# Gated linear attention into a star-ReLU feed-forward layer: two sets of PSUM banks for the attention blocks, and another listed order

## The chip, the core and the metric

The kernel runs on one core of a Trainium2 chip. The metric is the device time of one execution in microseconds (us). A core has engines that run side by side, each with its own queue in order: TensorE (PE in the profile, its weight loads PEld), VectorE (DVE), ScalarE (ACT), GpSimd (POOL), and SyncE (SP), which here issues nearly all DMAs. TensorE writes its products to PSUM, which has eight banks of 512 float32 per partition; VectorE and ScalarE read them from there.

## The reference

Two parts follow one another. The first is a recurrence over 768 tokens for 4 batches and 8 heads of 48 channels; the second is a feed-forward layer over the 3072 tokens of the first one's output.

```python
for t in range(S):
    state = alpha[:, :, t, :, None] * state + np.einsum('bhd,bhe->bhde', k[:, :, t], v[:, :, t])
    y[:, :, t] = np.einsum('bhd,bhde->bhe', q[:, :, t], state)

x = y.transpose(0, 2, 1, 3).reshape(B * S, H * D)      # 3072 x 384
h = x @ w_in                                           # 384 x 2048
r = np.maximum(h, 0.0)
g = s * (r * r) + b
out = g @ w_out                                        # 2048 x 384
```

## The kernel before

The tokens are cut into 24 blocks of 128 (`NBLK`), six to a batch (`NCH`). The recurrence is computed in chunks: within a block as a masked product of all queries with all keys, across blocks through a state. Blocks 0 to 5 (`windowed`) use a variant with half-blocks; the others go through these steps, each a small function that takes the number n of a block:

- `ln`, `cum`, `ex`: the logarithm of alpha, its running sum over tokens as a product with a triangle (bank `ct_ps`), and its exponentials. `qm` and `km` multiply q and k by them (VectorE).
- `trd`: one DMA for two blocks that transposes q and k into `qkT`. Before block 8, `tr` and `cp` do it on TensorE and VectorE.
- `amat` (L343): the products of keys and queries. Four pairs of heads, two products each with 48 rows of the array (rows 0 to 47 and 64 to 111), into the two banks `a_ps0` and `a_ps1`: eight products of 128 columns.
- `am` (L351): VectorE multiplies the two banks by the mask (`am_a`, then `am_b`).
- `ya` (L392, eight products) and `yi` (L366, four): y from the masked products and v, and from the state `sd` of the block before, summed in bank `y_ps`. `yev` copies y out.
- `sp` (L417, four products into bank `p_ps`), `t1` (L459, VectorE), `sd` (L469) and `sc` (L475, GpSimd): the state. `t1` adds the block's k and v products to `sc` of the block before; `sd` and `sc` multiply by the block's decay, which `last_row` and `decay` bring by two DMAs through DRAM. `sd` is two instructions, and the listed order says whether GpSimd (p) or VectorE (v) runs them.
- `xt` and `xev` transpose y for the second part by TensorE and a copy; from block 18 on `xtd` does it by DMA.
- `mp` (L500, a quarter of w_in: 12 products of 128 columns into one of two banks `h_ps`), `rl` (L514, ScalarE), `sq` (L521, VectorE), `o` (L536, four products of 384 columns into `o_ps`), `oev` (copy or L553 with the bias), `add_bias` (L588) and `store`: the second part. `mp n u` has the quarters u = 0 to 3, `o n u` too.
- `load x n` brings 128 tokens of q, k, v or alpha (a); `vcast` turns v to bfloat16. `colsum`, `bias_sum`, `bias_row` (L190) prepare the bias.

The last word of a step `sd`, `oev`, `yev`, `xev` and `vcast` names the engine: a for ScalarE, v for VectorE, p for GpSimd; without it, `yev` and `xev` run on ScalarE.

The order of all this is written out by hand, as one string `order` of 1096 steps. Each engine runs its instructions in the order of that list, and waits by semaphores for what it needs: a bank is written again only when its last readers are done, and SyncE issues its DMAs in the order of the list as well. Steps `busy` at the start multiply a mask by itself.

The banks are eight: `ct_ps`, `a_ps0`, `a_ps1`, `y_ps`, `p_ps`, `h_ps0`, `h_ps1`, `o_ps`. All blocks share the first five:

```python
    yw_ps = [y_ps, p_ps]
    pst = p_ps[:, 0:NP * 96].rearrange("a (p e) -> a p e", p=NP)
```

So `amat n+1` writes the banks that `am n` reads.

Of the kernel before, what the change touches and what calls it, by code (L numbers as in the profile page):

```python
# [14 lines left out]
def kernel(  # L15
# [14 lines left out]
    B, H, S, D = q.shape  # L30
# [30 lines left out]
    pst = p_ps[:, 0:NP * 96].rearrange("a (p e) -> a p e", p=NP)  # L61
# [265 lines left out]
    def amat(n):  # L327
        qkT = qkT_sb[n % 4]
        for p in range(NP):
# [5 lines left out]
            for g, e in tiles:  # L335
                r = slice(64 * e, 64 * e + 48)
                if g is None:
                    o, kT, qT = a_ps[e][:, p, :], qkT[r, 1, p, :], qkT[r, 0, p, :]
                else:
                    o = a_ps[e][HP * g : HP * g + HP, p, :]  # L340
                    kT = qkT[r, 1, 2 * g + i, HP * t : HP * t + HP]
                    qT = qkT[r, 0, 2 * g + i, :]
                nc.tensor.matmul(out=o, lhsT=kT, rhs=qT, start=True, stop=True)  # L343

    def am(n):
        for e in range(2):
            o, x, m = am_sb[e][n % 2], a_ps[e], mask4
# [10 lines left out]
    def yi(n):  # L358
        if n % NCH == 0:
            return  # L360
        for p in range(NP):
            if windowed(n):
                qT = qkT_sb[(n // 2 * 2 + p // 2) % 4][0:112, 0, 2 * (n % 2) + p % 2, :]
            else:
                qT = qkT_sb[n % 4][0:112, 0, p, :]
            nc.tensor.matmul(  # L366
                out=yw_ps[n % 2 * windowed(n)][:, 96 * p : 96 * p + 96],
# [7 lines left out]
    def ya(n):  # L375
# [15 lines left out]
        for h in range(H):  # L391
            nc.tensor.matmul(  # L392
                out=y_ps[:, 48 * h : 48 * h + 48],
# [7 lines left out]
    def sp(n):  # L401
# [13 lines left out]
        elif n % NCH < NCH - 1:  # L415
            for p in range(NP):
                nc.tensor.matmul(  # L417
                    out=pst[:, p, :],
# [6 lines left out]
    def yev(n, eng="a"):  # L425
        copy(eng, y_bf[n % 2], yw_ps[n % 2 * windowed(n)][:, 0 : H * 48])
# [22 lines left out]
    def t1(n):  # L449
# [3 lines left out]
        new = pst[0:112]  # L453
        if windowed(n):
            new = a_ps[n % 2].rearrange("a p t -> a (p t)")[0:112, 0 : NP * 96].rearrange("a (p e) -> a p e", p=NP)
# [5 lines left out]
    def sd(n, eng="p"):  # L461
# [3 lines left out]
        if eng == "s":  # L465
            src = a_ps[n % 2].rearrange("a p t -> a (p t)")[:, 0 : NP * 96].rearrange("a (p e) -> a p e", p=NP)
# [177 lines left out]
    def win(i, kk, eng):  # L644
# [129 lines left out]
```

## Time and profile before

| | us |
|---|---|
| median of 3 runs | 187.05 (186.97 to 188.03) |
| the profiled execution | 186.14 |
| its span, first to last instruction | 184.4 |
| TensorE busy | 176.8 |
| VectorE busy | 141.8 |
| ScalarE busy | 116.6 |
| GpSimd busy | 48.3 |

The page of the profile gives busy times, the span in 40 slices, the chain that ended last, and groups of instructions by line. The timeline lists instructions: start, length, engine, line, what is written and read, how many were merged; in square brackets stands idle time ahead of it and what ended that. A row with x12 runs from the first start to the last end. The table of stages gives busy time of each engine in a stretch of the span.

### The profile page before, as it was taken

To read this page: it belongs to the slowest core of one execution; us is meant where nothing else is said; L and a number is where in the kernel's file an instruction comes from. 1 tells how busy PE (TensorE), PEld (TensorE's weight loads), DVE (VectorE), ACT (ScalarE), POOL (GpSimd) and SP (SyncE) were. 2 spreads that over 40 slices of the span, in tenths; PEclk is the share of its full clock that TensorE was granted. 3 is DMA by queue.
4 is the path that set the end of the run, shared out by engine and by line. 5 is a ranking of instruction groups with operands and counts; after the bars stand their busy time and mean duration, and the time that the engine had idled before them with its cause. 6 is when DMAs were issued, how large, how long until landed. Compare 5 with 4: busy or idle time off the path is not lost.

```text
span 184.4 us, 6035 instructions
## 1 busy us (share of the span) xinstructions
PE 176.8 (96%) x2490; PEld 141.9 (77%) x2490; DVE 141.8 (77%) x301; ACT 116.6 (63%) x241; POOL 48.3 (26%) x80
## 2 busy tenths in 40 slices
PE   6998989999999999999999999999999999999992
PEld 4887879866788878788788788767777887878871
DVE  5487878887969979997687799997991983875161
ACT  2676869965579777887657869766427744533420
POOL 7124836000215182203373030322510202120000
PEclk9999999999999999999999999999999999999999
DMA  5999999989989999989799999997998889546252
GB/s 145 261 315 323 314 257 362 357 192 186 170 167 161 177 159 160 188 149 185 137 203 125 206 176 200 142 211 133 196 190 158 146 205 159 115 149 192 91 171 87
DMA packets 122162, 35.13 MB, mean 190 GB/s; under 512 B 115341, under 2 KB 120589, under 8 KB 122134
## 3 DMA queue, kind: packets, MB, share of 16 engines
q1 hardware_dynamic: 122130, 34.75, 92.9%
q8 instruction: 19, 0.31, 0.7%
q14 instruction: 9, 0.07, 0.2%
q10 hardware_dynamic: 4, 0.00, 0.0%
HBM read 25.20 MB, written 4.76 MB: 162 GB/s over the span
## 4 chain that ended last, share of the span: by engine, by line
PE 61%; SPq 12%; DVE 12%; DMA 10%; issue 2%; ACT 0%; DVEq 0%
PE o_ps L536 24%; PE h_ps L500 23%; SPq L148 8%; DMA w_out_st<-in_moe_w_out_dram 5%; DMA qkT<-qk_sb 4%; SPq L154 4%; PE a_ps L536 3%; PE a_ps L343 3%; DVE qk_sb L273 2%; DVE gt_all L521 2%; PE y_ps L392 2%; DVE am_b L351 2%; DMA k_sb<-in_k_dram 2%; DVE qk_sb L281 2%; DVE w_in_st L588 1%
## 5 line engine op out<-in xcount | busy, mean ns | idle before, releaser
L514 ACT ACTIVATE r_sb<-h_ps 128x512 bf16<-128x512 f32 x94 | 55.7, 598 | 32.9 <-PE h_ps L500 28.4
L500 PE MATMUL h_ps<-xd_all,w_in_bf 128*128 128x128 bf16 x1128 | 75.2, 219 | 0.8 <-issue 0.8
L500 PEld LDWEIGHTS <-w_in_bf 128*128 128x128 bf16 x1152 | 68.2, 98 | 5.9 <-issue 1.1
L536 PE MATMUL o_ps<-w_out_bf,gt_all 128*128 128x384 bf16 x336 | 63.5, 326 | 0.0
L536 PEld LDWEIGHTS <-gt_all 128*128 128x128 bf16 x368 | 33.6, 98 | 18.2 <-issue 0.2
L521 DVE TENSOR_TENSOR gt_all<-r_sb 128x512 bf16<-128x512 bf16 x96 | 39.7, 450 | 5.3 <-ACT r_sb L514 5.3
L469 POOL TENSOR_TENSOR sd_sb<-t_sb,blast_all 48x192 bf16<-48x192 f32 x26 | 15.7, 604 | 49.1 <-DVE t_sb L459 25.7
L475 POOL TENSOR_TENSOR sc_sb<-t_sb,blast_all 112x384 f32<-112x384 f32 x16 | 16.6, 1034 | 18.7 <-DVE t_sb L459 12.6
L315 POOL CAST v_bf<-v_sb 128x384 bf16<-128x384 f32 x13 | 8.1, 628 | 39.0 <-DMA v_sb<-in_v_dram 38.8
L273 DVE TENSOR_TENSOR qk_sb<-k_sb,bi_sb 128x384 bf16<-128x384 f32 x24 | 14.1, 590 | 5.1 <-ACT bi_sb L251 4.5
L351 DVE TENSOR_TENSOR am_a<-a_ps,mask 128x512 bf16<-128x512 f32 x18 | 12.3, 683 | 6.4 <-PE a_ps L343 6.1
L281 DVE TENSOR_TENSOR qk_sb<-q_sb,b_pair 128x384 bf16<-128x384 f32 x24 | 14.6, 613 | 1.0 <-DMA q_sb<-in_q_dram 0.8
L207 ACT ACTIVATE la_sb<-a_sb 128x384 bf16<-128x384 f32 x24 | 12.2, 524 | 2.6 <-DMA a_sb<-in_alpha_dram 2.6
L198 PE MATMUL o_ps<-mask 128*128 128x256 bf16 x78 | 12.4, 298 | 1.5 <-DVE mask L611 1.5
L313 ACT ACTIVATE y_bf<-y_ps 128x384 bf16<-128x384 f32 x21 | 10.3, 492 | 5.1 <-issue 2.3
L553 DVE TENSOR_TENSOR out_sb<-o_ps,bias_w 128x384 f32<-128x384 f32 x10 | 5.5, 554 | 9.2 <-PE o_ps L536 9.1
L351 DVE TENSOR_TENSOR am_b<-a_ps,mask 128x512 bf16<-128x512 f32 x18 | 12.2, 678 | 0.0
L251 ACT ACTIVATE bi_sb<-ct_ps 128x384 f32<-128x384 f32 x20 | 9.8, 491 | 3.6 <-PE ct_ps L227 3.2
L343 PE MATMUL a_ps<-qkT 48*128 48x128 bf16 (+1 forms) x240 | 10.1, 220 | 0.5 <-DVE am_b L351 0.3
L198 PEld LDWEIGHTS <-mask 128*128 128x128 bf16 x78 | 7.7, 107 | 3.2 <-DVE mask L611 1.5
L252 ACT ACTIVATE b_pair<-ct_ps 128x384 f32<-128x384 f32 x20 | 9.9, 496 | 0.0
L313 ACT ACTIVATE xd_all<-h_ps 128x384 bf16<-128x384 bf16 x13 | 6.4, 494 | 4.9 <-PE h_ps L432 4.9
(124 smaller groups left out, 209.1 us busy)
## 6 DMA issues: line engine op xcount, KB each, us to landing
a_sb<-in_alpha_dram SPq DMA_DIRECT2D x18, 192.0 KB, 4.4
q_sb<-in_q_dram SPq DMA_DIRECT2D x18, 192.0 KB, 4.4
k_sb<-in_k_dram SPq DMA_DIRECT2D x18, 192.0 KB, 3.8
v_sb<-in_v_dram SPq DMA_DIRECT2D x18, 192.0 KB, 4.8
w_in_st<-in_moe_w_in_dram SPq DMA_DIRECT2D x4, 768.0 KB
w_out_st<-in_moe_w_out_dram SPq DMA_DIRECT2D x4, 768.0 KB, 12.0
out_dram<-out_sb SPq DMA_DIRECT2D x10, 192.0 KB, 2.0
out_dram<-w_in_st SPq DMA_DIRECT2D x7, 192.0 KB, 2.1
```

The lines of the kernel that those rows point to most:

```text
L198: nc.tensor.matmul(out=o_ps[:, 0:n], lhsT=mask4[:, 0], rhs=mask4.rearrange("a p t -> a (p t)")[:, 0:n], start=True, stop=True,)
L273: nc.vector.tensor_tensor(out=by_head(kb_sb[n % 4][:, :, 0:48], n), in0=by_token(rows("k", n), n), in1=by_head(bi_sb[n % 2], n), op=ALU.mult,)
L281: nc.vector.tensor_tensor(out=by_head(qb_sb[n % 4][:, :, 0:48], n), in0=by_token(rows("q", n), n), in1=by_head(b_sb[n % 4][:, :, 0:48], n) ...
L313: nc.scalar.activation(out=out, in_=in_, func=AF.Copy)
L343: nc.tensor.matmul(out=o, lhsT=kT, rhs=qT, start=True, stop=True)
L351: nc.vector.tensor_tensor(out=o, in0=x, in1=m, op=ALU.mult)
L469: (nc.gpsimd if eng == "p" else nc.vector).tensor_tensor(out=sd_sb[n % 2][r, :, d], in0=src[r, :, d], in1=bl[r].to_broadcast([48, NP, 48]) ...
L475: nc.gpsimd.tensor_tensor(out=sc_sb[0:112], in0=t1_sb[0:112], in1=blast[n % 4][0:112].to_broadcast([112, NP, 96]), op=ALU.mult,)
L500: nc.tensor.matmul(out=hp[:, jj * N : (jj + 1) * N], lhsT=w_in_bf[:, kk, 128 * j : 128 * (j + 1)], rhs=xd_sb[g][:, kk, 0:N], start=(kk == ...
L514: nc.scalar.activation(out=rs, in_=h_of.pop((g, u)), func=AF.Relu)
L521: nc.vector.tensor_tensor(out=gt_sb[g][:, u * 512 : (u + 1) * 512], in0=rs, in1=rs, op=ALU.mult)
L536: nc.tensor.matmul(out=op[:, 0:d_model], lhsT=gt_sb[g][:, j * C : (j + 1) * C], rhs=w_out_bf[:, j, :], start=(j == 0), stop=(j == NJ - 1),)
```

## The change

The blocks from 6 on get their banks by parity. `bank(n, i)` is `a_ps0` or `a_ps1` for an even block and `y_ps` or `p_ps` for an odd one. The two halves of a block's masked products go to `bank(n, 0)` and `bank(n, 1)`; when `am` has read them, y is summed in `bank(n, 0)` (`y_of`) and the state's products go to `bank(n, 1)` (`state_of`). The windowed blocks keep their banks. The list of steps is the same up to `vcast 4 p; sq 0 2`, and another order from there on; the steps are the same 1096 apart from the engine named in 32 of them (`vcast`, `sd`, `oev`, `yev`, `xev`).

```diff
--- before.py
+++ after.py
@@ -58,7 +58,7 @@
     y_ps = ps.tile([128, 512], FP32, name="y_ps")
     p_ps = ps.tile([128, 512], FP32, name="p_ps")
     yw_ps = [y_ps, p_ps]
-    pst = p_ps[:, 0:NP * 96].rearrange("a (p e) -> a p e", p=NP)
+    a_flat = [t.rearrange("a p t -> a (p t)") for t in a_ps]
     h_ps = [ps.tile([128, 512], FP32, name=f"h_ps{i}") for i in range(2)]
     o_ps = ps.tile([128, 512], FP32, name="o_ps")
 
@@ -127,6 +127,16 @@
     def windowed(n):
         return n < NWIN
 
+    def bank(n, i):
+        return (yw_ps if n % 2 and not windowed(n) else a_flat)[i]
+
+    def y_of(n):
+        return yw_ps[n % 2] if windowed(n) else bank(n, 0)
+
+    def state_of(n):
+        t = bank(n, n % 2 if windowed(n) else 1)
+        return t[:, 0 : NP * 96].rearrange("a (p e) -> a p e", p=NP)
+
     def by_token(t, n):
         return t.rearrange("a (h t) d -> a t h d", t=2) if windowed(n) else t
 
@@ -335,7 +345,7 @@
             for g, e in tiles:
                 r = slice(64 * e, 64 * e + 48)
                 if g is None:
-                    o, kT, qT = a_ps[e][:, p, :], qkT[r, 1, p, :], qkT[r, 0, p, :]
+                    o, kT, qT = bank(n, e)[:, 128 * p : 128 * p + 128], qkT[r, 1, p, :], qkT[r, 0, p, :]
                 else:
                     o = a_ps[e][HP * g : HP * g + HP, p, :]
                     kT = qkT[r, 1, 2 * g + i, HP * t : HP * t + HP]
@@ -344,7 +354,7 @@
 
     def am(n):
         for e in range(2):
-            o, x, m = am_sb[e][n % 2], a_ps[e], mask4
+            o, x, m = am_sb[e][n % 2], bank(n, e).rearrange("a (p t) -> a p t", p=NP), mask4
             if windowed(n):
                 o, x = (z.rearrange("a (x i) t -> a x i t", x=2) for z in (o, x))
                 m = maskw.rearrange("a x (o t) s -> a x o (t s)", o=1).to_broadcast([128, 2, 2, 128])
@@ -364,7 +374,7 @@
             else:
                 qT = qkT_sb[n % 4][0:112, 0, p, :]
             nc.tensor.matmul(
-                out=yw_ps[n % 2 * windowed(n)][:, 96 * p : 96 * p + 96],
+                out=y_of(n)[:, 96 * p : 96 * p + 96],
                 lhsT=qT,
                 rhs=sd_sb[(n - 1) % 2][0:112, p, :],
                 start=(p == 0 and not windowed(n)),
@@ -390,7 +400,7 @@
             return
         for h in range(H):
             nc.tensor.matmul(
-                out=y_ps[:, 48 * h : 48 * h + 48],
+                out=y_of(n)[:, 48 * h : 48 * h + 48],
                 lhsT=am_sb[h % 2][n % 2][:, h // 2, :],
                 rhs=v_bf[n % 3][:, h, :],
                 start=(n % NCH == 0 and h == 0),
@@ -415,7 +425,7 @@
         elif n % NCH < NCH - 1:
             for p in range(NP):
                 nc.tensor.matmul(
-                    out=pst[:, p, :],
+                    out=state_of(n)[:, p, :],
                     lhsT=kb[:, 128 * p : 128 * p + 128],
                     rhs=v_bf[n % 3][:, 2 * p : 2 * p + 2, :],
                     start=True,
@@ -423,7 +433,7 @@
                 )
 
     def yev(n, eng="a"):
-        copy(eng, y_bf[n % 2], yw_ps[n % 2 * windowed(n)][:, 0 : H * 48])
+        copy(eng, y_bf[n % 2], y_of(n)[:, 0 : H * 48])
 
     def xt(n):
         hp = h_ps[nrelu[0] % 2].bitcast(BF16)[:, 0 : KT * C]
@@ -450,9 +460,7 @@
         c = n % NCH
         if c == NCH - 1:
             return
-        new = pst[0:112]
-        if windowed(n):
-            new = a_ps[n % 2].rearrange("a p t -> a (p t)")[0:112, 0 : NP * 96].rearrange("a (p e) -> a p e", p=NP)
+        new = state_of(n)[0:112]
         if c == 0:
             nc.vector.tensor_copy(out=t1_sb[0:112], in_=new)
         else:
@@ -463,7 +471,7 @@
             return
         bl, src = blast[n % 4], t1_sb
         if eng == "s":
-            src = a_ps[n % 2].rearrange("a p t -> a (p t)")[:, 0 : NP * 96].rearrange("a (p e) -> a p e", p=NP)
+            src = state_of(n)
         for e in range(2):
             r, d = slice(64 * e, 64 * e + 48), slice(48 * e, 48 * e + 48)
             (nc.gpsimd if eng == "p" else nc.vector).tensor_tensor(
@@ -675,67 +683,67 @@
         mp 1 3; rl 3 1; wout 0 2 v; sq 2 1; mp 0 3; sq 2 2; rl 1 3; sq 1 3; load_w_out 4 8; sq 3 0; wout 2 4 a; mp 2 3;
...
-        wout 12 16 v; o 2 2; o 1 2; o 2 3; o 1 3; oev 1 a; load_w v 2; vcast 4 p; sq 0 2; oev 2 v; o 0 2; sq 3 3; amat 4;
-        cum 6; sq 0 3; o 0 3; mp 3 2; ex 6; am 4; ya 4; amat 5; load q 6; yi 4; oev 0 a; qm 6; vcast 5 a; load k 6; km 6;
...
+        wout 12 16 v; o 2 2; o 1 2; o 2 3; o 1 3; oev 1 a; load_w v 2; vcast 4 p; sq 0 2; load k 6; colsum 4; sq 0 3;
+        load a 7; load q 6; oev 2 v; vcast 5 v; sq 3 3; mp 3 2; rl 3 2; amat 4; am 4; cum 6; o 0 2; o 0 3; oev 0 a; amat 5;
...
-        o 5 0; o 5 1; o 5 2; rl 6 1; load v 9; cum 11; ex 11; vcast 9 a; trd 8; mp 7 2; amat 8; rl 7 2; decay 8; sq 6 2;
-        load q 11; yi 8; t1 8; o 5 3; load k 11; oev 5 a; am 8; sc 8; sq 6 1; sp 9; sq 6 3; mp 7 1; rl 7 1; colsum 6;
-        amat 9; ya 8; km 11; yev 8; mp 7 0; rl 7 0; mp 7 3; rl 7 3; sd 8 p; qm 11; o 6 0; xt 8; xev 8; yi 9; o 6 1; sq 7 1;
...
+        qm 10; last_row 8; oev 5 v; rl 6 2; xev 7; mp 7 3; ex 11; mp 7 2; trd 8; load v 8; vcast 8 p; amat 8; load k 11;
+        amat 9; rl 7 3; mp 7 0; qm 11; rl 7 2; rl 7 0; mp 7 1; rl 7 1; am 8; yi 8; ya 8; yev 8; o 6 0; sq 6 1; o 6 1;
+        sq 6 2; load k 10; xt 8; sq 7 0; sq 7 2; km 10; ln 12; cum 12; km 11; load k 13; last_row 10; sq 7 1; sc 7; sq 7 3;
+        sp 8; xev 8; t1 8; o 6 2; decay 8; sd 8 p; mp 8 3; o 6 3; rl 8 3; sc 8; am 9; mp 8 1; rl 8 1; ex 12; mp 8 0; yi 9;
...
-        mp 15 2; sp 16; km 18; ex 20; rl 14 1; vcast 18 p; add_bias 6; sq 14 3; qm 19; trd 16; add_bias 1; amat 16;
-        decay 16; o 13 0; mp 15 1; cum 21; km 19; sc 15; load q 21; am 16; amat 17; load v 17; yi 16; ya 16; rl 15 2;
...
+        sq 13 1; o 12 3; xev 15; trd 16; amat 16; amat 17; last_row 16; mp 15 1; rl 15 1; mp 15 3; am 16; sp 16; sd 15 p;
+        load k 19; yi 16; ya 16; mp 15 0; sc 15; load q 19; km 19; qm 19; rl 15 3; cum 20; sq 14 3; load v 18; oev 12 a;
...
```

107 lines of the change are left out of this document (53 added, 54 removed).

## Prediction

> **What bounds the kernel now.** I read the page first (busy shares, slices), then the table of stages, then TensorE's timeline instruction by instruction, and last VectorE and the DMA queue around the masked products.
>
> ```profile
> span 184.4 us, 6035 instructions
> PE 176.8 (96%) x2490; PEld 141.9 (77%) x2490; DVE 141.8 (77%) x301; ACT 116.6 (63%) x241; POOL 48.3 (26%) x80
> PE   6998989999999999999999999999999999999992
> 50.00:70.00 20.00, 19.91 (x287) 16.46 (x284) 17.22 (x33) 15.44 (x33) 8.29 (x9) 1.00 0.96 168
> 70.00:90.00 20.00, 20.00 (x288) 16.21 (x286) 18.93 (x41) 15.56 (x32) 3.77 (x6) 1.00 1.06 163
> 90.00:110.00 20.00, 19.82 (x284) 15.99 (x282) 15.32 (x33) 13.99 (x30) 7.41 (x10) 1.00 1.04 175
> 110.00:130.00 20.00, 19.72 (x263) 15.07 (x261) 18.86 (x39) 13.42 (x30) 4.72 (x7) 1.00 1.13 175
> 130.00:150.00 20.00, 19.97 (x271) 15.47 (x270) 15.92 (x34) 11.35 (x23) 3.79 (x6) 1.00 0.95 182
> 150.00:170.00 20.00, 20.00 (x283) 16.36 (x282) 12.71 (x30) 8.91 (x16) 2.74 (x5) 1.00 0.70 155
> ```
>
> The columns of a stage are its length, then busy time of TensorE, weight loads, VectorE, ScalarE, GpSimd, the granted clock, the share of the 16 DMA engines, GB/s. TensorE is full from 50 to 170 (119.4 of 120 us) at clock 1.00. The change keeps every multiplication, so the end can move in two ways only: TensorE needs less time for the same products, or it waits more or less. VectorE is second (99.0 of 120 us from 50 to 170, and 18.9 of 20 in two stages), and the DMA engines are near full up to 150.
>
> "Busy" hides lost time, because one product is drawn about 0.2 us long though the next starts long before its end. So I compare starts:
>
> ```profile
> 55.89 0.81 PE L536 MATMUL o_ps<-w_out_bf,gt_all 128*128 128x384 bf16 x4
> 56.54 0.33 PE L227 MATMUL ct_ps<-la_sb,U_bf 128*128 128x384 bf16 x1
> 57.35 0.83 PE L500 MATMUL h_ps<-xd_all,w_in_bf 128*128 128x128 bf16 x12
> 58.11 0.40 PE L343 MATMUL a_ps<-qkT 48*128 48x128 bf16 x8
> 58.44 1.51 PE L500 MATMUL h_ps<-xd_all,w_in_bf 128*128 128x128 bf16 x24
> 59.79 0.33 PE L417 MATMUL p_ps<-v_bf,qk_sb 128*128 128x96 bf16 x4
> ```
>
> Twenty-four h products take 59.79 - 58.44 = 1.35 us, so a step `mp` of 12 is 0.67; a step `o` is 56.54 - 55.89 = 0.65. The `mp` ahead of the eight products of `amat 7` takes 58.11 - 57.35 = 0.76, 0.09 more than its work. `amat` itself holds TensorE for 58.44 - 58.11 = 0.33. Its eight products, each about 0.22 long, lie within 0.40, so their starts are (0.40 - 0.22) / 7 = 0.026 apart and they feed for 8 x 0.026 = 0.21; the next step starts 0.12 later. One lone `amat` thus costs 0.09 + 0.33 = 0.42 us, of which 0.21 is work and 0.21 a gap at its two ends.
>
> **The change, part by part.** *Banks.* From block 6 on, an even block has its two masked-product banks, its y and its state in `a_ps0`/`a_ps1`, an odd block in `y_ps`/`p_ps`. In the new order the products of blocks (8,9), (10,11), (12,13), (14,15), (16,17), (19,18), (20,21), (23,22) stand directly behind one another on TensorE: eight pairs; in the old one no such pair is adjacent. The second of a pair starts in the mode of the first, so one exit and one entry fall away: 0.12 + 0.09 = 0.21 us each, 8 x 0.21 = 1.7 us, all of it on TensorE's own path. The trace has no adjacent pair of this shape; bounds are 0 (the gap comes back inside the pair) and 0.33 + 0.09 = 0.42 a pair, 3.4 us, if the second were free, which its 0.21 of feeding excludes. I take 1.7.
>
> The Trainium skill ("TensorEngine Tiling (Array Packing)", Key Properties) says that changing the tiling mode drains the array, while changing the tile does not; the gaps of 0.09 and 0.12 us at 58.11 agree, and by that rule the pair keeps no gap inside, the same 1.7 us.
>
> *Waits that go.* Four places where TensorE lost time:
>
> ```profile
> 47.51 0.50 PE L408 MATMUL a_ps<-v_bf,qk_sb 64*128 64x96 bf16 x16
> 48.26 0.34 PE L227 MATMUL ct_ps<-la_sb,U_bf 128*128 128x384 bf16 x1 [0.24 <-DVE qkT L318]
> 61.64 0.19 PE L392 MATMUL y_ps<-v_bf,am_a 128*128 128x48 bf16 x1
> 61.92 0.20 PE L392 MATMUL y_ps<-v_bf,am_b 128*128 128x48 bf16 x1
> 91.21 0.81 PE L536 MATMUL o_ps<-w_out_bf,gt_all 128*128 128x384 bf16 x4
> 92.20 0.40 PE L343 MATMUL a_ps<-qkT 48*128 48x128 bf16 x8 [0.18 <-DMA qkT<-qk_sb]
> 121.81 0.23 PE L343 MATMUL a_ps<-qkT 48*128 48x128 bf16 x1
> 122.32 0.38 PE L343 MATMUL a_ps<-qkT 48*128 48x128 bf16 x7 [0.28 <-DVE am_b L351]
> ```
>
> At 121.81 the second product of `amat 17` starts 0.51 later, not 0.03: it waits until `am 16` has read `a_ps1`. With two bank pairs this wait cannot occur: 0.49 gained. At 61.64 `ya 7` waits 0.25 (0.28 less 0.03) for `am_b`; the old order has 3.2 us of TensorE work between `amat 7` and `ya 7`, the new one 5.2. At 48.26 `cum 7` waits 0.24 for `cp 6`; now `xt 4`, `o`, `mp` (1.5 us) lie between `tr 6` and `cum 7`. Together 1.0 us; lower bound 0 if VectorE is later by as much. At 92.20 `amat 12` waits for the transposing DMA of its operands (91.21 + 0.65 + 0.09 = 91.95, so 0.25 lost); I leave that as it is:
>
> ```profile
> 85.01 3.72 SPq L306 DMA_TRANSPOSE qkT<-qk_sb  x1
> 89.40 0.55 SPq L142 DMA_DIRECT2D a_sb<-in_alpha_dram  x1
> 90.00 1.02 SPq L142 DMA_DIRECT2D k_sb<-in_k_dram  x1
> ```
>
> These are SyncE's issues and what each takes there. `trd 12` is issued at 85.01 and used at 92.20. TensorE will reach `amat 12` about 0.9 us earlier (0.42 from two pairs, 0.5 from the waits), while `trd 12` has 42 instead of 44 steps ahead of it on SyncE's queue since the common part, 1.1 to 2.0 us at 0.55 to 1.02 each, so the two moves cancel or better. The other seven `trd` have 0, +1, -2, -4, 0, -1 and +1 steps; no DMA is added.
>
> *Waits that come.* `yi n` and `ya n` write the bank that `am_a` reads, and `sp n` the bank that `am_b` reads; before, `sp` ran up to 10 us ahead of the products. What `am` needs:
>
> ```profile
> 142.63 0.40 PE L343 MATMUL a_ps<-qkT 48*128 48x128 bf16 x8
> 143.06 0.69 DVE L351 TENSOR_TENSOR am_a<-a_ps,mask 128x512 bf16<-128x512 f32 x1 [3.88 <-PE a_ps L343]
> 143.67 0.68 DVE L351 TENSOR_TENSOR am_b<-a_ps,mask 128x512 bf16<-128x512 f32 x1
> 60.59 0.68 DVE L351 TENSOR_TENSOR am_a<-a_ps,mask 128x512 bf16<-128x512 f32 x1
> ```
>
> With VectorE free, `am_a` ends 143.75 - 142.63 = 1.12 us after the first product, `am_b` 144.35 - 142.63 = 1.72. In the new order a pair takes 0.33 + 0.21 = 0.54 and then: blocks 8 and 10 two `mp` and `yi` (`ya` at 0.54 + 1.34 + 0.17 = 2.05 against 1.72), blocks 16 and 20 two `mp` (`sp` at 1.88 against 1.72), block 14 one `mp` (`yi` at 1.21 against 1.12). The room is 0.33, 0.33, 0.16, 0.16 and 0.09 us. VectorE is busy 82% of the time with instructions of about half a microsecond, so `am` comes some 0.2 late on average: five waits of about 0.1, 0.5 us, which is my value. Bounds: 0, and eight times the lag of `am 7` (60.59 - 58.11 = 2.48 against 0.43, 2.05 late) less 0.2 of room, 14.8 us.
>
> *Engines of copies.* From the common part on, VectorE has three `sd` more (six instructions), three `vcast` fewer, one `oev` fewer, and one `xev` for a `yev`:
>
> ```profile
> L469 DVE TENSOR_TENSOR sd_sb<-t_sb,blast_all 48x192 bf16<-48x192 f32 x10 | 4.7, 470 | 0.1
> L469 POOL TENSOR_TENSOR sd_sb<-t_sb,blast_all 48x192 bf16<-48x192 f32 x22 | 13.0, 592 | 49.0 <-DVE t_sb L459 25.7 <-PE y_ps L366 15.6 <-PE h_ps L500 3.7
> L475 POOL TENSOR_TENSOR sc_sb<-t_sb,blast_all 112x384 f32<-112x384 f32 x12 | 13.1, 1095 | 16.5 <-DVE t_sb L459 11.6 <-DMA blast_all<-row_dr 4.8
> L459 DVE TENSOR_TENSOR t_sb<-p_ps,sc_sb 112x384 f32<-112x384 f32 x12 | 6.6, 552 | 3.0 <-PE p_ps L417 1.5 <-POOL sd_sb L469 1.4
> L315 DVE CAST v_bf<-v_sb 128x384 bf16<-128x384 f32 x5 | 1.8, 352 | 0.0
> L553 DVE TENSOR_TENSOR out_sb<-o_ps,bias_w 128x384 f32<-128x384 f32 x10 | 5.5, 554 | 9.2 <-PE o_ps L536 9.1
> ```
>
> That is 6 x 0.470 - 3 x 0.352 - 0.554 + about 0.15 = +1.4 us on VectorE. The cover is its idle fifth; if it were full, these 1.4 us would lie on the path. ScalarE gains about 1 us, GpSimd loses two; neither is near its limit.
>
> *Sum.* 0 (work) - 1.7 (pairs) - 1.0 (waits that go) + 0.5 (waits that come) = -2.2 us. The profiled execution took 186.14 us, 1.74 around its span; its new time would be 183.9, the span 182.2. The median of the runs shown is 0.91 higher, 187.05, so I predict 187.05 - 2.2 = 184.8 us.
>
> **The rivals.** *The gain is handed back.* VectorE lags by half a microsecond more at the eight pairs, or the DMA queue is late at `amat 12` and two more: eight waits of 0.2 us more, or three of 0.6, cost about 1.7, and the time is 184.85 + 1.7 = 186.6. For it: 18.9 of 20 us busy at 70 to 90 and 110 to 130, and the room of 0.09 to 0.33 us. Against it: where the next step depended on it, as at 142.63, `am` began at once.
>
> The Trainium skill ("TensorEngine Tiling (Array Packing)", PSUM Bottleneck) warns that tiling speeds up TensorE but not the evacuation of PSUM, which may become the limit. That speaks for this rival: four masked products of 0.6 us each (143.67 - 143.06) now fall due together; the old trace shows no such four.
>
> *The change doesn't do what it says.* The gap is tied to each group of eight and stays inside the pair. Then only -1.0 + 0.5 remains: 186.6. Against it: the entry gap stands before the first of eight, and between the eight there is none.
>
> *Slower: the state's recurrence becomes the bound.* `sp n` now follows `am n`, so `sp n`, `t1 n` (0.55), `sd n` (2 x 0.59), `yi n+1` is a short chain, with `sc n` (1.10) on GpSimd ahead of `t1 n+1`. It needs 0.55 + 1.18 = 1.7 us and handoffs; the new order leaves 3.3 us of TensorE work between `sp 8` and `yi 9`, 4.2 to 8.4 at the other blocks; in the old order it is 2.8 at block 22, 3.2 at block 4 and 5 to 23 elsewhere. It decides once VectorE is 1.5 us behind at `t1`, as it was by 2.05 at `am 7`. If `am` and `t1` are both late by that at four pairs, each costs 2.05 - 0.2 at `ya` or `sp`: 4 x 1.85 = 7.4, less the 2.7 gained, and the time is 187.05 + 4.7 = 191.8. Against it: only at block 8 is there less than 4 us, and `am` of the even blocks has not been late by that (143.06).
>
> **How the numbers follow.** Forecast 0.55, gain handed back 0.22, gap stays 0.08, recurrence 0.15. 1% of this kernel (1.9 us) is about what a measurement can tell from no change. The forecast of -2.2 lies beyond it, at -1.2%; the two middle cases lie within it, 0.30. So faster 0.55, same 0.30, slower 0.15. Range: below, the pairs' 1.7, the 1.0, the 0.25 at 92.20 and no new wait give 184.1; with 0.9 of scatter, as between the profiled execution and the median, 183.2. Above, it takes in the two middle cases and the mild end of the last, two late pairs in place of four: 187.05 - 2.7 + 3.7 = 188.1.
>
> **What would show it.** Right: on TensorE's timeline eight groups of 16 products of 48 rows that hold 0.54 us up to the next start; no wait of L343's successor on `am_b`; the stages from 50 to 170 shifted earlier by 0.2 us per pair. The waits that come would stand before `yi`, `ya` or `sp` of blocks 8, 10, 14, 16 and 20, under 0.3 us each. Wrong: a pair that holds 0.75 us; waits of TensorE on VectorE, GpSimd's `sd` or the transposing DMA that sum to over 2 us; a clock below 1.00.

## The result and the profile after

| | us |
|---|---|
| changed kernel, median of 6 runs | 184.75 (183.96 to 186.01) |
| kernel before beside it, median of 6 runs | 187.01 (186.43 to 188.33) |
| ratio | 0.9885, 95% interval 0.9843 to 0.9926 |
| profiled execution of the changed kernel | 184.97 |
| its span | 183.2 |

The changed kernel is faster by 1.1%, 2.3 us. A single execution of either kernel strays by 1 us and more about its median, so the ratios carry the verdicts below and the profiles the reasons: the two profiled executions lie only 1.2 us apart. The ratios leave out slow executions, those over 1.5% above the fastest of their kernel (three of ten where the pairs are parted below), so they can differ from the quotient of the medians.

From the page of the changed kernel, and its table of stages (the columns are those of before):

```profile
span 183.2 us, 6055 instructions
PE 175.7 (96%) x2490; PEld 142.1 (78%) x2490; DVE 140.9 (77%) x303; ACT 116.6 (64%) x243; POOL 51.1 (28%) x76
110.00:130.00 20.00, 20.00 (x285) 16.03 (x283) 16.18 (x37) 15.28 (x34) 6.17 (x8) 1.00 1.18 178
130.00:150.00 20.00, 19.58 (x278) 15.71 (x277) 17.76 (x38) 10.91 (x22) 4.89 (x6) 1.00 0.90 188
150.00:170.00 20.00, 18.10 (x237) 14.16 (x235) 11.88 (x28) 8.68 (x17) 0.94 (x1) 1.00 0.74 158
```

TensorE is as full as before until 130 us, and then is not: 18.1 of 20 us from 150 to 170, where it was full before. VectorE has not become the limit there (11.9 of 20), nor has the clock dropped.

The pair of blocks 8 and 9 on TensorE's timeline, and VectorE's `am 8` behind it:

```profile
68.59 0.40 PE L353 MATMUL a_ps<-qkT 48*128 48x128 bf16 x8
68.83 0.22 PE L353 MATMUL y_ps<-qkT 48*128 48x128 bf16 x1
69.14 1.51 PE L508 MATMUL h_ps<-xd_all,w_in_bf 128*128 128x128 bf16 x24
70.67 0.19 PE L402 MATMUL a_ps<-v_bf,am_a 128*128 128x48 bf16 x1
69.03 0.69 DVE L361 TENSOR_TENSOR am_a<-a_ps,mask 128x512 bf16<-128x512 f32 x1 [0.62 <-PE a_ps L353]
69.63 0.68 DVE L361 TENSOR_TENSOR am_b<-a_ps,mask 128x512 bf16<-128x512 f32 x1
```

The first product of block 9 (`y_ps`, 68.83) starts 0.24 us after the first of block 8, and the pair holds TensorE for 69.14 - 68.59 = 0.55 us. `am_b` ends at 70.31 and the first `ya 8` starts at 70.67, without a wait.

Where TensorE does wait now, from its view of waits, and the same places on its timeline:

```profile
PE y_ps L353 <- DMA qkT<-qk_sb: 1.0, 1, 1.0
PE y_ps L376 <- DVE sd_sb L477: 0.8, 1, 0.8
PE p_ps L427 <- ACT v_bf L323: 0.4, 1, 0.4
147.32 0.81 PE L544 MATMUL o_ps<-w_out_bf,gt_all 128*128 128x384 bf16 x4
148.56 0.33 PE L427 MATMUL p_ps<-v_bf,qk_sb 128*128 128x96 bf16 x4 [0.42 <-ACT v_bf L323]
153.73 0.81 PE L544 MATMUL o_ps<-w_out_bf,gt_all 128*128 128x384 bf16 x4
155.54 0.23 PE L353 MATMUL y_ps<-qkT 48*128 48x128 bf16 x1 [1.00 <-DMA qkT<-qk_sb]
161.93 0.83 PE L508 MATMUL h_ps<-xd_all,w_in_bf 128*128 128x128 bf16 x12
163.60 0.33 PE L376 MATMUL y_ps<-sd_sb,qkT 112*128 112x96 bf16 x4 [0.84 <-DVE sd_sb L477]
```

By starts, `sp 21` loses 148.56 - 147.32 - 0.65 = 0.59 us, `amat 23` (first of the pair 23, 22) 155.54 - 153.73 - 0.65 = 1.16, of which 0.09 is the entry gap, and `yi 23` 163.60 - 161.93 - 0.67 = 1.00. What they wait for comes from SyncE:

```profile
144.08 1.25 SPq L152 DMA_DIRECT2D v_sb<-in_v_dram  x2
149.25 3.71 SPq L316 DMA_TRANSPOSE qkT<-qk_sb  x1
154.93 2.52 SPq L591 DMA_DIRECT2D out_dram<-w_in_st  x4
157.50 0.59 SPq L588 DMA_DIRECT2D out_dram<-w_in_st  x1
158.13 1.11 SPq L591 DMA_DIRECT2D out_dram<-w_in_st  x2
159.34 0.54 SPq L277 DMA_DIRECT2D blast_all<-row_dr  x1
162.83 0.72 DVE L477 TENSOR_TENSOR sd_sb<-t_sb,blast_all 48x192 bf16<-48x192 f32 x2 [1.71 <-DMA blast_all<-row_dr]
```

`decay 22` is issued at 159.34 behind seven store instructions that took 154.93 to 159.24; VectorE stands 1.71 us for it, and TensorE stands behind VectorE. `trd 22` is issued at 149.25 and takes 3.71 us, and the two loads of v issued from 144.08 on are those of blocks 21 and 22.

I summed over the stretch from 30 to 190 us what each product's start lags the one before beyond its work; where a change of shape falls on a wait, only the usual 0.10 us of an entry or 0.12 of an exit is counted as the change. In us of TensorE: the changes between masked products and others 4.4 before (40 of them), 2.6 after (24); the waits that went (`amat 17` 0.48, `ya 7` 0.25, `cum 7` 0.42, `trd 12` 0.25) 1.4 and 0; `sp 21`, `amat 23`, `yi 23` and the step behind it 0 and 2.9; smaller ones make up the rest of a balance of -0.8. TensorE's last product ends 0.7 us earlier.

### The profile page after: what moved, and what is told of

It is laid out like the page before. It is cut to its first block, busy times and chain, and to the rows that moved or that the text cites. A ratio compares the mean times of both kernels' runs of the same rounds, so it can differ in the third digit from the quotient of the medians.

```text
span 183.2 us, 6055 instructions
## 1 busy us (share of the span) xinstructions
PE 175.7 (96%) x2490; PEld 142.1 (78%) x2490; DVE 140.9 (77%) x303; ACT 116.6 (64%) x243; POOL 51.1 (28%) x76
## 4 chain that ended last, share of the span: by engine, by line
PE 73%; DVE 8%; DMA 6%; SPq 6%; issue 3%; ACT 2%; DVEq 0%; ACTq 0%
PE h_ps L508 26%; PE o_ps L544 23%; PE o_ps L208 4%; PE a_ps L544 3%; SPq L591 3%; PE a_ps L353 3%; DMA qkT<-qk_sb 2%; DMA v_sb<-in_v_dram 2%; DVE sd_sb L477 2%; DMA blast_all<-row_dr 2%; PE h_ps L442 2%; PE ct_ps L237 1%; PE a_ps L572 1%; SPq L588 1%; DVE qk_sb L291 1%
## 5 line engine op out<-in xcount | busy, mean ns | idle before, releaser
L529 DVE TENSOR_TENSOR gt_all<-r_sb 128x512 bf16<-128x512 bf16 x96 | 38.3, 434 | 5.4 <-ACT r_sb L522 5.2
L477 POOL TENSOR_TENSOR sd_sb<-t_sb,blast_all 48x192 bf16<-48x192 f32 x20 | 18.7, 935 | 22.8 <-DVE t_sb L467 11.8
L325 POOL CAST v_bf<-v_sb 128x384 bf16<-128x384 f32 x15 | 9.3, 630 | 51.0 <-DMA v_sb<-in_v_dram 48.6
L483 POOL TENSOR_TENSOR sc_sb<-t_sb,blast_all 112x384 f32<-112x384 f32 x16 | 15.2, 953 | 21.5 <-DVE t_sb L465 13.0
L291 DVE TENSOR_TENSOR qk_sb<-q_sb,b_pair 128x384 bf16<-128x384 f32 x24 | 13.9, 580 | 2.4 <-ACT b_pair L262 2.2
L208 PE MATMUL o_ps<-mask 128*128 128x256 bf16 x78 | 13.5, 317 | 1.5 <-DVE mask L619 1.5
L361 DVE TENSOR_TENSOR am_a<-a_ps,mask 128x512 bf16<-128x512 f32 x9 | 6.2, 692 | 4.8 <-PE a_ps L353 4.7
L477 DVE TENSOR_TENSOR sd_sb<-t_sb,blast_all 48x192 bf16<-48x192 f32 x18 | 8.1, 451 | 1.9 <-DMA blast_all<-row_dr 1.7
L323 ACT ACTIVATE y_bf<-y_ps 128x384 bf16<-128x384 f32 x12 | 5.9, 491 | 5.6 <-DVE out_sb L561 3.7
L353 PEld LDWEIGHTS <-qkT 48*128 48x128 bf16 (+1 forms) x240 | 5.8, 99 | 3.9 <-issue 1.5
```

What stands on the lines that cost most here:

```text
L208: nc.tensor.matmul(out=o_ps[:, 0:n], lhsT=mask4[:, 0], rhs=mask4.rearrange("a p t -> a (p t)")[:, 0:n], start=True, stop=True,)
L291: nc.vector.tensor_tensor(out=by_head(qb_sb[n % 4][:, :, 0:48], n), in0=by_token(rows("q", n), n), in1=by_head(b_sb[n % 4][:, :, 0:48], n) ...
L323: nc.scalar.activation(out=out, in_=in_, func=AF.Copy)
L477: (nc.gpsimd if eng == "p" else nc.vector).tensor_tensor(out=sd_sb[n % 2][r, :, d], in0=src[r, :, d], in1=bl[r].to_broadcast([48, NP, 48]) ...
L483: nc.gpsimd.tensor_tensor(out=sc_sb[0:112], in0=t1_sb[0:112], in1=blast[n % 4][0:112].to_broadcast([112, NP, 96]), op=ALU.mult,)
L529: nc.vector.tensor_tensor(out=gt_sb[g][:, u * 512 : (u + 1) * 512], in0=rs, in1=rs, op=ALU.mult)
```

## The experiments

Theory: the gap at the change of shape falls away eight times (1.7 us), and late transfers in SyncE's order eat a part of it. Rivals: the other banks or the other order does it without the adjacency; VectorE is at its limit and hands the gain back. Edits of the listed order are shown as steps taken out and put in.

**The changed kernel again.** No edit.

> The changed kernel once more, as the measure for the others on the same chip. Its six runs lay between 183.96 and 186.01 us, so 184.0 to 186.0 is expected. Theory: its late waits (the transposing DMA ahead of the products of block 23, 1.2 us by starts; the state of block 22 ahead of yi 23, 1.0; v of block 21, 0.6) stand again in the profile, since they come from the listed order. Rival: they belong to that one execution; then their sum of 2.7 us falls below 1.5 here.

Measured: 185.46 us (183.63 to 186.91, 10 runs) beside 187.22, ratio 0.9887 [0.985, 0.9925]. The gain holds, and the late waits at blocks 21 to 23 stand again, 3.6 us by starts. (The profiled execution took 186.91 us, the longest of the ten, so the size of these waits is not set against others.)

**Pairs parted.** All banks and steps as changed; one step of TensorE between the two products of each pair:

```diff
-amat 8; load k 11; amat 9; rl 7 3; mp 7 0;
+amat 8; load k 11; rl 7 3; mp 7 0; amat 9;
...
```

> The changed kernel with one step of ordinary products (an mp, once an xt) put between the two masked products of each of the eight pairs; banks and the rest of the order stay. Theory: TensorE pays for entering and leaving the mode of 48 rows, so each split costs 0.21 us again, 8 x 0.21 = 1.7 us, and the timeline shows eight rows more that hold 0.33 us and 0.09 us ahead of each. Rival 1: the pair saved nothing by being adjacent, and the gain came from the order and the banks: the time stays within 0.4 us. Rival 2: the odd blocks' products come 0.7 us later and make am wait: over 2.5 us.

TensorE's timeline at blocks 8 and 9:

```profile
68.67 0.40 PE L353 MATMUL a_ps<-qkT 48*128 48x128 bf16 x8
69.00 0.84 PE L508 MATMUL h_ps<-xd_all,w_in_bf 128*128 128x128 bf16 x12
69.78 0.23 PE L353 MATMUL y_ps<-qkT 48*128 48x128 bf16 x1
70.11 0.84 PE L508 MATMUL h_ps<-xd_all,w_in_bf 128*128 128x128 bf16 x12
```

70.11 - 68.67 - 0.67 = 0.77 us against 0.55: 0.22 a pair. Over the stretch from 30 us on the changes of shape cost 4.4 us against 2.6, +1.8. The median is 186.08 (184.01 to 187.18, 10 runs), ratio 0.9904 [0.9864, 0.9943]: 0.6 us above the changed kernel beside it, between the theory's 1.7 and the first rival's 0.4, and the intervals overlap. The profiles, 1.3 us apart, show a part of the reason: TensorE comes later to blocks 21 to 23, and the late waits shrink from 2.9 to 2.1 us. The gap is shown; its full worth in the time is not.

**Old banks, the odd product behind `am`.** `bank`, `y_of` and `state_of` give every block the banks of before, and the odd block's product comes directly behind `am` of the even one in the list:

```diff
 def bank(n, i):
-    return (yw_ps if n % 2 and not windowed(n) else a_flat)[i]
+    return a_flat[i]
...
-amat 8; load k 11; amat 9; rl 7 3; mp 7 0; ... rl 7 1; am 8; yi 8;
+amat 8; load k 11; rl 7 3; mp 7 0; ... rl 7 1; am 8; amat 9; yi 8;
...
```

> The changed kernel's order with the old banks: all blocks from 6 on use a_ps0 and a_ps1 for products, y_ps for y and p_ps for the state; so that the one pair of banks suffices, the products of a pair's odd block are listed directly behind am of its even block. Theory: the gain of 2.3 us is the pairs' 1.7 and waits that go 1.3, less new waits in the last 40 us; without pairs 1.7 comes back, and the odd products wait for am_b of the even block, about 1.72 us after its first product, with 1.3 to 2.0 us of other work between: 0 to 0.4 us each, 1 us together: 2 to 3 us slower than the changed kernel, so about as before. Rival: the new order by itself is the gain and banks matter only by letting pairs in: 1.5 us slower or less. Second rival: the odd products stand behind a late VectorE: over 4 us slower.

```profile
79.71 0.40 PE L353 MATMUL a_ps<-qkT 48*128 48x128 bf16 x8
80.89 0.21 PE L353 MATMUL a_ps<-qkT 48*128 48x128 bf16 x1 [0.78 <-DVE am_a L361]
81.49 0.38 PE L353 MATMUL a_ps<-qkT 48*128 48x128 bf16 x7 [0.39 <-DVE am_b L361]
```

Measured: 189.61 us (189.35 to 189.79), ratio 1.0124 [1.0096, 1.0152], slower than before, and 4.2 us above the changed kernel beside it, where 2 to 3 had been expected. At four pairs (10, 12, 14, 20) no step of TensorE lies between the two, and each costs 0.97 + 0.57 us: the product cannot start until `am_a` has read its bank, and goes on only behind `am_b`. I had expected other work to cover part of it; at those four there was none. This placement mixes the banks with its own waits, so:

**Old banks, pairs 1.3 us of work apart.** As above, the odd product at least 1.3 us of TensorE's work behind the even one.

```diff
-amat 10; am 10; amat 11; rl 8 2; ... mp 9 2; rl 9 2; qm 13; mp 9 1; colsum 7;
+amat 10; am 10; rl 8 2; ... mp 9 2; rl 9 2; qm 13; mp 9 1; amat 11; colsum 7;
...
```

> The changed kernel's order with the old banks, once more: the products of a pair's odd block now stand behind at least 1.3 us of other work after those of the even block, in all eight pairs (in the run before, four of them followed at once and waited 1.5 us each, 6.1 us together). Theory A, order and pairs: the banks serve to let the pairs stand together and nothing else; against the changed kernel the split costs 1.7 us and waits for am_b (due 1.72 us after the first product, work 1.3 to 2.0 us) 0 to 0.4 us a pair, 1.5 us at most: 1.7 to 3.2 us slower, 186.5 to 188.5. Theory B, the banks free more than that (y and state of neighbours no longer share a bank): over 4 us slower.

```profile
68.62 0.40 PE L353 MATMUL a_ps<-qkT 48*128 48x128 bf16 x8
70.39 0.40 PE L353 MATMUL a_ps<-qkT 48*128 48x128 bf16 x8
```

Measured: 186.30 us (184.98 to 187.52, 10 runs), ratio 0.9964 [0.9926, 1.0002]. No product waits for a bank, and the changes of shape cost 4.4 us. Against the changed kernel run again (185.46 us, 0.9887) that is slower by 0.8 us by the medians and by 1.4 by the ratios, and the two intervals do not quite touch: pairs, with the banks that allow them, are worth something in the time too. It is the time of the parted pairs within 0.2 us, though the ratios of the two (0.9904 and 0.9964) leave room for 1 us. In this order the other banks earn nothing that is seen except that pairs may stand together.

**New banks in the old order.** The list of before, with `yi`, `sp` and `t1` moved behind `am` for the blocks where they stood ahead of it; block 10, for one:

```diff
-trd 10; yi 10; amat 10; am 10; rl 9 0;
+trd 10; amat 10; am 10; yi 10; rl 9 0;
...
```

> The new banks in the kernel of before's order; only where the banks demand it, yi, sp and t1 of blocks 7 to 11, 13, 16 and 19 are set behind am of their block. No pair is adjacent. Theory: without pairs the switching costs are those of before, the wait of amat 17 for am 16 (0.5 us) goes, and the moved yi and sp wait for am at five or six blocks, 0.3 to 1 us each: 0 to 4 us slower than before, 187 to 191. Rival: parity of the banks is a gain in itself, by waits that nothing in the profile names: faster than before by 1 us or more.

TensorE's view of waits (us in total, times, longest):

```profile
PE a_ps L427 <- POOL v_bf L325: 1.6, 1, 1.6
PE p_ps L427 <- DVE am_b L361: 1.5, 2, 1.1
PE a_ps L427 <- DVE am_b L361: 1.3, 2, 0.6
PE a_ps L376 <- DVE am_a L361: 1.1, 1, 1.1
```

Measured: 191.80 us (191.21 to 192.03), ratio 1.0258 [1.0213, 1.0304]. `sp` and `yi` stand behind `am` with nothing between: 3.9 us by this view, 4.8 by starts, and 1.8 more by starts where `sp` meets a late cast of v. So the new banks put `am` on the path of the state, as the prediction's slower rival said, and only the new order keeps it off.

**A late `am`.** VectorE copies 128x384 out of the bank ahead of `am` of blocks 8, 10, 14, 16 and 20, the five for which I had priced a wait:

```diff
+    def pad(n):
+        nc.vector.tensor_copy(out=pad_sb, in_=bank(n, 0)[:, 0:d_model])
...
-rl 7 1; am 8;
+rl 7 1; pad 8; am 8;
```

> The changed kernel with one copy of 128x384 values out of the product bank put on VectorE directly ahead of am of blocks 8, 10, 14, 16 and 20 (0.47 to 0.55 us each; its output is not used). Theory, the room of the prediction: at 8 and 10 TensorE has 0.33 us of room, at 16 and 20 0.16, at 14 0.09; so it waits 0.15 to 0.2, 0.15 to 0.2, 0.4, 0.3 and 0.3 us ahead of yi, ya or sp, 1.3 us together, in the timeline. Rival: VectorE has its own slack there and TensorE waits under 0.4 us in all; second rival: VectorE is the limit and the five copies cost their full 2.4 us or more.

Block 14, TensorE and VectorE:

```profile
105.05 0.84 PE L513 MATMUL h_ps<-xd_all,w_in_bf 128*128 128x128 bf16 x12
106.14 0.34 PE L381 MATMUL a_ps<-sd_sb,qkT 112*128 112x96 bf16 x4 [0.25 <-DVE am_a L361]
104.93 0.56 DVE L366 COPY pad_sb<-a_ps 128x384 f32<-128x384 f32 x1 [0.42 <-PE a_ps L353]
```

Measured: 185.6 us in one run. The five waits by starts are 0.14, 0.14, 0.41 (106.14 - 105.05 - 0.67), 0.33 and 0.34: 1.36 us. So the room of 0.09 to 0.33 us was worked out rightly. Without the copies, in the profile of the changed kernel, VectorE was never late there: the rival in which it hands the gain back is excluded for these blocks of that execution.

**Stores out of the way.** Eight stores of old blocks that stood ahead of late loads on SyncE are moved back:

```diff
-load q 23; store 6; ... store 3; ... store 9; ... store 12; ... store 2; ... store 1; ... store 11; ... store 0;
+store 19; store 6; store 3; store 9; store 12; store 2;
+store 20; store 1; store 11; store 0;
```

> The changed kernel with eight stores of results kept from early blocks (3, 6, 9, 12 and 0, 1, 2, 11: twelve DMAs of some 0.6 us on SyncE's queue) moved from ahead of the last transposing DMA and the last decay to behind the last xtd. Theory: the three late waits are these steps' place in SyncE's queue; the last transposing DMA is issued about 4 us earlier, the last decay about 7 us earlier, the waits of 1.2, 1.0 and 0.6 us go, and the time falls by 2.0 to 2.7 us against the changed kernel. Rival: the transfers are late because the DMA engines are full, or another wait follows at once (the xtd of block 22, the results' buffers at the end): the time falls by less than 0.8 us.

TensorE at `amat 23` and SyncE:

```profile
153.73 1.14 PE L544 MATMUL o_ps<-w_out_bf,gt_all 128*128 128x384 bf16 x6
154.81 0.23 PE L353 MATMUL y_ps<-qkT 48*128 48x128 bf16 x1
147.92 2.02 SPq L316 DMA_TRANSPOSE qkT<-qk_sb  x1
153.40 0.52 SPq L277 DMA_DIRECT2D blast_all<-row_dr  x1
```

Measured: 184.10 us (182.38 to 184.44), ratio 0.9809 [0.9747, 0.987], 1.4 us below the changed kernel beside it, short of the 2.0 to 2.7 expected. `decay 22` is issued 5.9 us earlier, and the three late waits are gone (under 0.1 us each). New waits stand in this execution: `trd 12` and `trd 20` made TensorE wait 0.9 and 1.2 us.

**The same, with loads behind `trd 12`.** `load q 14` and `load a 15` moved behind `trd 12`, `store 14` behind `trd 20`, to take those two waits away.

```diff
-load q 14; vcast 12 a; load a 15; trd 12;
+vcast 12 a; trd 12; load q 14; load a 15;
...
-store 14; mp 18 1; trd 20;
+mp 18 1; trd 20; store 14;
```

> The kernel with the eight stores moved, and two more steps of SyncE: two loads (q of block 14, alpha of block 15) behind the transposing DMA of block 12, and the store of block 14 behind that of block 20. Theory: what TensorE still waits for in that kernel are these two transposing DMAs (0.9 us at the products of block 12, 1.2 at block 20); issued 1.5 and 0.5 us earlier, they give back 0.9 and 0.5: 1.4 us less than the kernel with the eight stores moved, 182.0 to 183.5. Rival: the transposing DMAs land late because transfers already under way share the DMA engines, and the waits move or stay: within 0.7 us of it.

```profile
90.91 0.52 ACT L217 ACTIVATE la_sb<-a_sb 128x384 bf16<-128x384 f32 x1 [2.74 <-DMA a_sb<-in_alpha_dram]
91.87 0.21 PE L353 MATMUL y_ps<-qkT 48*128 48x128 bf16 x1 [1.75 <-ACT y_bf L323]
```

Measured: 184.59 us (184.28 to 186.16), ratio 0.989 [0.9847, 0.9932]: a miss. The profile is of the longest of the six executions, 186.16 us. In it ScalarE stands at `ln 15` for the late alpha, `yev 11` is queued behind it, and `amat 13` needs the bank that `yev 11` empties: 1.9 us. The `trd` came sooner and the load it was moved past came too late.

**Stores out of the way, again and with other steps past the `trd`.** The first is the kernel of moved stores once more; in the second `last_row 12` goes behind `trd 12` and `store 14` behind `trd 20`.

```diff
-last_row 12; xev 10; ... load a 15; trd 12;
+xev 10; ... load a 15; trd 12; last_row 12;
...
-store 14; mp 18 1; trd 20;
+mp 18 1; trd 20; store 14;
```

> The kernel with the eight stores moved, once more, for its time (its four runs: 182.4 to 184.4 us) and a second profile. Theory: the late waits at the products of block 23, at yi 23 and at sp 21 are gone again (under 0.3 us in all), since they come from SyncE's order; what is left are waits for the transposing DMAs of blocks 12 and 20, which differ from run to run between 0 and 1.3 us; median 183.5 to 184.5. Rival: it was chance: late waits of over 1 us at block 21 to 23 stand here too.

> The kernel with the eight stores moved, and the row of block 12 and the store of block 14 set behind the transposing DMAs of blocks 12 and 20, which nothing on TensorE waits for soon; no load is moved. (In the kernel with two loads moved as well, alpha of block 15 came late, ScalarE stood 2.7 us at its logarithm with the copy of y 11 behind it, and the products of block 13 waited 1.9 us.) Theory: the transposing DMAs are issued 0.4 to 0.5 us earlier each and TensorE's waits for them fall by as much: 0 to 0.9 us less than the kernel with the eight stores moved. Rival: no difference, since those waits come from transfers that share the DMA engines.

Measured: 183.31 us (182.05 to 184.99), ratio 0.9782 [0.9727, 0.9837], and 183.88 (182.02 to 185.38), ratio 0.9844 [0.979, 0.9898]: no difference that can be told. The late waits at blocks 21 to 23 are gone in both profiles, and TensorE waits for no `trd` longer than 0.2 us. In the first a new wait stands at the end, on VectorE, in the add of the last half:

```profile
177.04 0.88 SPq L588 DMA_DIRECT2D out_dram<-out_sb  x2
179.17 0.36 DVE L581 TENSOR_TENSOR out_sb<-a_ps,bias_w 128x192 f32<-128x192 f32 x1 [1.93 <-DMA out_dram<-out_sb]
```

TensorE was done 2.7 us earlier than in the changed kernel (177.5 against 180.2), but the span only 0.9 shorter: the add waits for the result buffer that `store 21` holds, which now stood behind the moved stores.

**Three of them and `store 8` behind `store 21`.**

```diff
-store 20; store 1; store 11; store 0; mp 23 3; store 8; ... store 21;
+store 20; mp 23 3; ... store 21; store 1; store 11; store 0; store 8;
```

> The order of the kernel with the late stores behind store 19 and 20, but the stores of blocks 1, 11, 0 and 8 put behind the store of block 21. In the profile of that kernel the add of the last half of the last block waited 1.93 us for a buffer of results that the store of block 21 held, issued at 177.04 us behind the moved stores; TensorE had ended at 177.5 us. Theory (the moved stores set the end by the buffer): the store of block 21 is issued some 2 us earlier, the last add no longer waits over 0.5 us, and the median lies 0.5 to 1.5 us below that kernel's 183.3 to 184.1, so 182 to 183. Rival (the last stores set the end in any order, since the four moved ones still stand ahead of the last two on the same queue): the wait goes but the last store is issued as late as before, and the median stays within 0.7 us of 183.7.

```profile
177.62 0.39 SPq L588 DMA_DIRECT2D out_dram<-out_sb  x1
178.81 0.36 DVE L581 TENSOR_TENSOR out_sb<-a_ps,bias_w 128x192 f32<-128x192 f32 x1 [0.30 <-PE a_ps L572]
143.07 0.40 PE L353 MATMUL a_ps<-qkT 48*128 48x128 bf16 x8 [1.20 <-DMA qkT<-qk_sb]
```

Measured: 182.38 us (182.03 to 183.67, 8 runs), ratio 0.9753 [0.9708, 0.9798]: faster than both kernels, and the interval lies apart from the changed one's. The last add waits for TensorE, no longer for the buffer. Against the kernel of the eight moved stores the intervals overlap. `amat 20` waited 1.4 us for `trd 20` here.

**Pairs parted in this order.** The steps are moved as where the pairs were parted first (`amat 8; load k 11; rl 7 3; mp 7 0; amat 9` and so on).

> The order with the nine stores moved (the median of that kernel was 182.38 us, ratio 0.9753), and in it the two masked products of each of the eight pairs parted by one step of TensorE, as in the earlier kernel with parted pairs. There parting cost 1.75 us at the changes of shape by the profile, but only 0.6 us in the median, while the waits for SyncE's late transfers at blocks 21 to 23 were shorter (2.1 us against 3.5). Theory (those waits had swallowed the difference, since the transfers come at their own time): with the stores out of the way the whole 1.7 us shows, the median is 183.8 to 184.4 and the ratio 0.983 to 0.986, with under 0.5 us of waits at blocks 21 to 23. Rival (the pairs are worth only 0.6 us in any order): 182.7 to 183.2, ratio 0.977 to 0.980.

```profile
143.22 0.40 PE L353 MATMUL a_ps<-qkT 48*128 48x128 bf16 x8
```

Measured: 184.14 us (183.64 to 184.86) beside 188.44, ratio 0.976 [0.9707, 0.9814]. The median falls where the theory put it, 1.8 us above that of the whole pairs, but the kernel before was slower by 1.1 us in this comparison too, and by the ratio, which is what may be compared, nothing was lost; 0.983 is excluded, the rival's 0.977 to 0.980 is not. No wait is left at blocks 21 to 23, as the theory said, and the changes of shape cost 4.4 us against 2.6. But the wait of 1.4 us at `amat 20` has gone: the kernel with whole pairs has its product of block 20 at 143.07, this one at 143.22. In these two executions, what the pairs had saved by then was spent waiting for the transposing DMA, and TensorE's last products end 0.6 us apart (178.8 and 179.4).

That does not settle the time. The execution with this wait took 183.64 us, and six of the eight of its kernel took only 182.03 to 182.68. The kernel with the eight stores moved, run again, has whole pairs too, and TensorE's timeline has no wait at block 20:

```profile
141.69 0.40 PE L353 MATMUL a_ps<-qkT 48*128 48x128 bf16 x8
```

TensorE's last product ends there at 177.5, 1.9 us ahead of the parted pairs. So what the eight pairs are worth in the time stays open, between nothing by the ratios and the whole gap by the medians. What the profiles show is that a late transfer in SyncE's order can take it back, at block 20 here, at 21 to 23 in the changed kernel.

## Why the prediction was right, point by point

The time was forecast as 187.05 - 2.2 = 184.8 us; it is 184.75, and the medians of the repeated comparison give -1.8. The sum is nearer than its terms.

*Pairs, -1.7.* Right as a mechanism and as a size on TensorE: 0.55 us held (0.54 predicted), 0.21 to 0.22 saved a pair, 1.8 for the eight when they are parted. In the time it is shown only in part. "The gap stays inside the pair" is excluded. The Trainium skill ("TensorEngine Tiling (Array Packing)", Key Properties) has a drain at a change of mode and none at a change of tile; the 16 products of a pair on two row tiles agree with it: block 9's first product starts 0.24 us after block 8's, of which 0.21 is work.

*Waits that go, -1.0.* Right in place, too small in size. `amat 17`, `ya 7` and `cum 7` are gone, the last with 0.42 rather than 0.24 us: I had read the bracket of the view of waits, which leaves out what is lost inside the drawn length of the product ahead. And the 0.25 at `trd 12`, which I left as it was, went in this execution: 1.4 in all.

*Waits that come, +0.5.* This is the step that failed. I placed them at `am` of blocks 8, 10, 14, 16 and 20; there are none in the profile. The room was right (the late `am` shows it), the lag of 0.2 us was not: an average lag from VectorE's busy share says little on an instruction that VectorE is waiting for. In their place stand 2.9 us in one execution at blocks 21 to 23, all in SyncE's order. I had counted the steps ahead of each `trd` but not priced `load v 21` and `decay 22`, nor asked which transfers a TensorE that is early would meet first. My own sign of failure, waits for the transposing DMA and for VectorE of over 2 us, was met (1.16 and 1.00 by starts), while the median still came out. In the two profiled executions it did not: they lie 1.2 us apart, not 2.2, since this term is 2.4 us larger and the others together 1.4 smaller. That the median hit to 0.1 us is partly luck.

*VectorE, +1.4 us.* Its instructions changed as counted (12 to 18 `sd` of this form, five `vcast` to two), but its busy time fell by 0.9, for one because the 96 squarings took 434 instead of 450 ns each. It did not bind.

*The rivals.* "Handed back" is right in kind for the DMA queue and wrong for VectorE: the warning of the Trainium skill ("TensorEngine Tiling (Array Packing)", PSUM Bottleneck) that draining PSUM may become the limit is not borne out here: behind a pair the four `am` products of 0.7 us each found room, and no wait of TensorE on them stands in the profile. "The recurrence" is a real danger of the new banks: it cost 4.8 us when the old order was kept, and nothing in the new one.

What stays open: why executions of one kernel differ by 1 to 3 us. Which `trd` is late (12, 20 or 22) changes from one to the next, and SyncE's issue of the same transpose takes 2 to 4 us; what sets that was not tried.

## What to carry to other kernels

Put products of the same array shape next to each other, and give them the banks for it: it saves TensorE 0.2 us each time on its timeline, if the readers of the banks have work of TensorE ahead of their dependants. Then read the issuing queue again for what an earlier TensorE meets, for stores ahead of a load, a transpose or a decay can turn the gain into waits; here moving stores that nobody awaits was worth as much as the change itself. A gain that is cashed in front of a fixed arrival is not yet a gain.

## What the hardware showed that was not expected

Each of the two instructions of a step `sd` on GpSimd was priced at 0.592 us. The same instruction takes 0.50 to 2.75 us in the changed kernel, by what VectorE does meanwhile. GpSimd, then VectorE:

```profile
77.42 2.75 POOL L477 TENSOR_TENSOR sd_sb<-t_sb,blast_all 48x192 bf16<-48x192 f32 x1 [1.13 <-DVE t_sb L467]
77.26 0.95 DVE L193 TENSOR_TENSOR cs_sb<-cs_sb,w_out_st 128x768 f32<-128x768 f32 x1
79.40 0.42 DVE L529 TENSOR_TENSOR gt_all<-r_sb 128x512 bf16<-128x512 bf16 x1
80.00 0.69 DVE L361 TENSOR_TENSOR am_a<-a_ps,mask 128x512 bf16<-128x512 f32 x1 [0.19 <-PE a_ps L353]
```

From 77.26 to 79.82 VectorE runs five instructions in a row on tiles of SBUF alone, and `sd` ends at 80.17, after they have. The second instruction of this `sd`, from 80.25 on beside `am`, which reads a bank of PSUM, takes 0.51. Another, at 64.22, took 2.62 us, 2.58 of it beside such a row. The Trainium skill ("SBUF — State Buffer", Who interferes with whom) says that a VectorE instruction with two inputs in SBUF contends with a GpSimd instruction that reads SBUF, and that the ports they share are an exclusive lock; the trace agrees. It cost nothing here, as TensorE did not wait for that `sd`.

The issue of one DMA on SyncE's queue is no small price: a load or store mostly took 0.4 to 1.1 us, and the same transpose `trd 22` 3.71 us in the changed kernel and 2.02 with the stores moved; nothing behind it is issued meanwhile.
